# Two of the four gate stages moved behind attention segments, with gated activations in a ring of three

## The chip, the cores and the metric

The kernel runs on one core of a Trainium2 chip. The metric is the device time of one execution in microseconds (us). Before the change the median of three runs is 283.71 us (283.68 to 283.90).

## The reference, cut to what matters

Two branches read the same input x (2048 tokens of 512 features, bf16). Branch A is an attention with 32 heads of 16 features over four segments of 512 tokens. Inside a segment it is causal softmax attention. Beside it stands a memory: segment s reads what the keys and values of the segments before it have added up. Branch B is a gated feed-forward layer of width 1792. A gate per token mixes the two.

```
phi = lambda t: where(t > 0, t + 1.0, exp(t))
for s in range(4):
    p = softmax(qs @ ks.T * scale + mask);  a_dot = p @ vs
    a_mem = (phi(qs) @ M) / (phi(qs) @ z + 1e-6)
    o = g * a_mem + (1 - g) * a_dot
    M = M + phi(ks).T @ vs;  z = z + phi(ks).sum()
a = concat(o) @ wo
b = (gelu(x @ w_gate) * (x @ w_up)) @ w_down
out = sigmoid(x . gate_w) * a + (1 - sigmoid(x . gate_w)) * b
```

## The kernel before, in words

All weights and the transposed input `xT` lie in SBUF for the whole run. The work is cut into 1,076 small tasks, and each task has a name. The string `ORDER` at the top of the file lists every task once, in the order in which it is issued; `Sched.run` walks it. An engine executes its own tasks in that order, and waits where a task needs a result or a buffer that another engine has not yet given. Nothing else sets the order. A suffix `@A` or `@D` puts a copy on ACT or DVE.

The names that the text uses, with s the segment, and c a group of eight heads:

- `gt s.p` (L320, through `gate_pair`): two blocks of x @ w_gate, eight matmuls of 128x512 into one PSUM tile of 2 banks. `egt s.p` (L487, ACT): gelu of that tile into `G`. There are 7 of each per segment.
- `up s.h` (L320, `up_group`): four matmuls of x @ w_up into one bank. `eup` (L497, DVE) multiplies it into `G` in place. 14 per segment.
- `k`, `q`, `v` (L320, L422): the projections, four matmuls each, with a copy to SBUF on ACT or DVE (`ek`, `eq`, `ev`). `ko` (L334) is a second, masked copy of k.
- `lg n` (L574): the logits of slot n. A segment has 20 slots (5 for each c), so n runs from 0 to 79. A slot writes two PSUM tiles of 2 banks. `ex n a` and `ex n b` (L597, ACT) take exp of each into the ring `pT` of 12; `as n a/b` (L606, POOL) zero the masked triangle.
- `pv s.c e/o` (L626): probabilities times values; `epv` (L644, DVE) transposes it out of PSUM; `r`, `rg`, `n`, `m`, `o` (L654 to L670, DVE) normalize it, add the memory part and put the result into `xT`, in the place of the input.
- `E`, `Q`, `Em`, `ph` (L690 to L701; ACT, DVE, DVE, POOL): phi of k or q. `pk` (L730, SP) transposes phi(k) by DMA, `M` (L739) updates the memory, `mbd` and `zbd` (L761, L764) lay it out. `den` (L780) and `num` (L810) read it; `eden`, `rma`, `rmr`, `rmg`, `enum`, `nm` (L790 to L823, DVE) finish that.
- `dn s.t.*` (L834): G @ w_down for 128 tokens, in three pieces of 5, 5 and 4 matmuls. `wo` (L839) adds the attention's output to the same PSUM bank, `os` (L879, L881) scales it, `st` (L844) stores it.
- `gz`, `egz`, `zsp`, `g2`, `omz`: the mixing gate of all tokens.

PSUM is shared by two rings. The ring `lg` has three tiles of 2 banks; it serves `gt`, `lg` and the `dn` of the last segment. The ring `gen` has two tiles of 1 bank; it serves all other matmul groups. A tile is taken in the order of ORDER, and its next user waits until its reader on ACT or DVE is done.

Before the change the order has three parts. First come the first segment's projections and all 28 `gt` with their gelus, padded with some `up`. The first `ex` names all gelus in its dependencies, so ACT passes from gelu to exp once. `G` is one tile for all four segments. The weights of the gate (`wga`) and one small tile lie in a pool `ph1` that is closed at the task `opened`; the rings `T` to `pk` then take its memory. Second come the 80 slots, with `up`, projections, memory work and `dn` between them. Third, behind `lg79`, come the rest of the `dn` and `wo`.

The loads are issued by SP at the start, in this order: x of segment 0, `wk`, `wq`, the first part of `wga`, `wv`, the rest of `wga`, x of segments 1 to 3 by DMA transposes (L234, four per segment), `gw`, `beta8`, `wup`, `wo`. `wdn` follows as the first task on SP, because x of segment 0 first uses its place.

Of the kernel before, what the change touches and what calls it, by code (L numbers as in the profile page):

```python
# [32 lines left out]
open xt0 xt1 ext0 xt2 ext1 xt3 ext2 k0f0 ext3 k0f1 k0f2 q0.0 k0f3 eq0.0@D q0.1 ek0.1@A ek0.2@D  # L33
ek0.0@A gt0.0 eq0.1@A ek0.3@A gt0.1 egt0.0 q0.2 egt0.1 gt0.6 eq0.2@D gt1.3 gt1.0 egt1.3 egt0.6
q0.3 egt1.0 gt0.5 gt2.3 v0.0 egt2.3 gt1.1 egt0.5 eq0.3@A gt2.1 egt1.1 wdn gt1.6 egt2.1 gt0.3
egt1.6 gt0.2 egt0.3 v0.2 egt0.2 gt1.4 gt3.5 egt1.4 ev0.0@A ev0.2@A gt1.5 up0.6 egt1.5 gt3.0 eup0.6
egt3.5 gwB up0.10 gt3.3 eup0.10 up0.3 egt3.3 bps gt2.2 eup0.3 egt3.0 ebps omg gt1.2 egt2.2 up0.7
up0.4 eup0.7 gt2.5 eup0.4 eb gz ko0.0 egt2.5 ko0.1 gt3.6 egt1.2 egz zsp gt3.1 egt3.6 up0.2 egt3.1
gt2.0 up0.5 gt0.4 eup0.5 eup0.2 gt3.2 egt0.4 egt2.0 up0.0 gt2.4 eup0.0 gt3.4 egt2.4 egt3.2 up0.8
egt3.4 up0.1 eup0.8 gt2.6 eup0.1 wos v0.1 egt2.6 opened v0.3 ev0.1@D lg0 ev0.3@D up0.12 ex0a up0.9  # L40
eup0.12 up0.11 eup0.9 Ek0.0 up0.13 eup0.11 ex0b lg1 Qk0.0 eup0.13 q1.0 ex1a Emk0.0 k1.0 phk0.0
eq1.0@D ex1b lg2 ek1.0@D k1.1 ex2a ko1.0 v1.2 as0b pk0.0 ek1.1@D ex2b as0a lg3 as2a ev1.2@D q1.1
ex3a as1a v1.1 as1b Ek0.1 eq1.1@D as3a v1.3 ev1.1@A Emk0.1 Qk0.1 g2 v1.0 phk0.1 ev1.3@A ex3b lg4
ev1.0@D up1.0 ex4a up1.2 as2b pk0.1 eup1.0 Eq1.0 as4a up1.1 eup1.2 as3b ex4b Emq1.0 pv0.0e eup1.1
as4b lg5 epv0.0e M0.0 ex5a Qq1.0 up1.3 eM0.0 phq1.0 ex5b lg6 eup1.3 pv0.0o ex6a up1.4 epv0.0o as5b
ex6b as5a r0.0 up1.5 eup1.4 as6a Ek1.0 lg7 as6b eup1.5 M0.1 ex7a Qk1.0 up1.6 Emk1.0 eM0.1 ex7b lg8
ko0.2 rg0.0 up1.7 eup1.6 ex8a mbd0 as7b up1.8 eup1.7 ex8b lg9 as7a eup1.8 up1.9 as8a ex9a as8b
pv0.1e phk1.0 eup1.9 ex9b lg10 epv0.1e k1.2 ex10a k1.3 as9b ek1.2@D pk1.0 ex10b as9a q1.2 ek1.3@D
as10b Ek1.1 lg11 as10a eq1.2@D pv0.1o n0.0 ex11a up1.10 epv0.1o ex11b lg12 as11a eup1.10 q1.3
Emk1.1 ex12a Qk1.1 up1.11 phk1.1 eq1.3@A lg13 ex12b eup1.11 up1.12 omz ex13a r0.1 up1.13 as12b  # L50
eup1.12 pk1.1 Eq1.1 as11b up2.0 eup1.13 as12a ex13b lg14 eup2.0 pv0.2e ex14a Emq1.1 up2.1 ko0.3
epv0.2e ex14b lg15 rg0.1 Qq1.1 up2.2 eup2.1 ex15a as14b o0.0 up2.3 as13b eup2.2 ex15b as13a lg16
as14a eup2.3 up2.4 ex16a n0.1 pv0.2o eup2.4 ex16b as16a lg17 epv0.2o up2.5 ex17a as16b r0.2 up2.6
rg0.2 zbd0 eup2.5 ex17b as17a lg18 as15a eup2.6 up2.7 ex18a as15b n0.2 as17b up2.8 eup2.7 ex18b
phq1.1 lg19 eup2.8 pv0.3e ex19a o0.1 up2.9 epv0.3e ex19b lg20 as18a eup2.9 up2.10 as18b ex20a o0.2
as19a up2.11 as19b eup2.10 ex20b lg21 eup2.11 pv0.3o ex21a as20b up2.12 epv0.3o ex21b as21a r0.3
lg22 eup2.12 as20a up2.13 ex22a rg0.3 n0.3 den1 ex22b as22a eup2.13 lg23 as21b eden1 k2.0 ex23a
as22b o0.3 pv1.0e rma1 ek2.0@A as23a rmr1 ex23b lg24 num1.0 epv1.0e ex24a as23b rmg1 k2.1 enum1.0
ex24b ko1.1 lg25 nm1.0 q2.0 ex25a as24b ek2.1@D as24a eq2.0@D num1.1 ex25b lg26 enum1.1 pv1.0o
ex26a nm1.1 epv1.0o num1.2 ex26b as26a lg27 enum1.2 q2.1 ex27a nm1.2 as26b dn0.0.0 Ek2.0 as25a  # L60
lg28 as25b ex27b dn0.0.5 Emk2.0 as27a Qk2.0 ex28a as27b dn0.0.10 ko1.2 eq2.1@A phk2.0 wo0.0 ex28b
lg29 os0.0@D num1.3 ex29a enum1.3 pv1.1e as28b Eq2.0 lg30 as28a epv1.1e v2.0 as29a ex30a r1.0
Emq2.0 v2.1 ev2.0@D ex29b Qq2.0 v2.2 ev2.1@D ex30b as29b lg31 ev2.2@D v2.3 ex31a ko2.0 rg1.0
pv1.1o ev2.3@D ex31b lg32 epv1.1o M1.0 ex32a as31b r1.1 dn0.1.0 pk2.0 n1.0 as31a ex32b rg1.1 lg33
dn0.1.5 ex33a m1.0 as32b ko1.3 as30a ex33b lg34 st0.0 n1.1 dn0.1.10 as30b ex34a eM1.0 wo0.1 as32a
ex34b as34a lg35 os0.1@D pv1.2e ex35a as34b k2.2 epv1.2e as33a ex35b as33b lg36 ek2.2@D phq2.0
pv1.2o ex36a k2.3 epv1.2o ex36b lg37 ek2.3@D q2.2 as35b ex37a o1.0 as36b q2.3 eq2.2@D as35a ex37b
as36a lg38 eq2.3@D M1.1 as37a ex38a r1.2 as37b dn0.2.0 ko2.2 Ek2.1 eM1.1 lg39 dn0.2.5 ex38b Qk2.1
rg1.2 Emk2.1 n1.2 ex39a dn0.2.10 as38b ex39b lg40 as39a wo0.2 as38a ex40a as39b pv1.3e os0.2@D
phk2.1 ex40b lg41 epv1.3e st0.2 pv1.3o st0.1 ex41a up3.0 epv1.3o ex41b lg42 as41a eup3.0 up3.1  # L70
ko2.1 ex42a as41b up3.2 eup3.1 ex42b as42a lg43 eup3.2 up3.3 as40b ex43a mbd1 as42b up3.4 r1.3
eup3.3 ex43b as40a lg44 eup3.4 as43a pv2.0e ex44a rg1.3 m1.1 up3.5 epv2.0e Eq2.1 as44a o1.1 lg45
dn0.3.0 ex45a nm1.3 n1.3 ex44b dn0.3.5 zbd1 Emq2.1 m1.3 ex45b m1.2 as44b lg46 Qq2.1 dn0.3.10 ex46a
as43b eup3.5 wo0.3 phq2.1 o1.3 ex46b lg47 os0.3@D pv2.0o ex47a o1.2 st0.3 up3.6 as45a epv2.0o
ex47b as46b lg48 r2.0 den2 as46a ex48a eup3.6 as47b eden2 as45b ex48b lg49 as47a k3.0 rma2 ex49a
pv2.1e ek3.0@D ex49b lg50 as49a rmr2 k3.1 ex50a epv2.1e as49b ek3.1@D as48a num2.0 ex50b lg51
as48b enum2.0 pv2.1o rmg2 ex51a nm2.0 epv2.1o num2.1 ex51b lg52 enum2.1 q3.0 ex52a ko2.3 nm2.1
q3.1 eq3.0@D ex52b as52a lg53 eq3.1@D as50b num2.2 ex53a as51a enum2.2 dn1.0.0 as51b rg2.0 ex53b
as50a nm2.2 lg54 as53a dn1.0.5 ex54a n2.0 ex54b lg55 as54a dn1.0.10 as52b ex55a wo1.0 as53b as54b
Eq3.0 lg56 as55a os1.0@D pv2.2e ex56a m2.0 pv2.2o ko3.0 epv2.2e ex55b as56a epv2.2o num2.3 ex56b  # L80
lg57 as55b enum2.3 v3.0 r2.1 ex57a rg2.1 v3.1 n2.1 ex57b as57a ev3.0@D lg58 as56b ev3.1@D v3.2
ex58a as57b o2.0 ex58b lg59 ev3.2@D pv2.3e r2.2 m2.1 ex59a v3.3 epv2.3e ex59b lg60 ev3.3@D M2.0
rg2.2 ex60a dn1.1.0 eM2.0 n2.2 ex60b as60a lg61 Emq3.0 dn1.1.5 as59a Qq3.0 ex61a as58a dn1.1.10
o2.1 ex61b as58b nm2.3 as59b lg62 wo1.1 ex62a ko3.1 as61b pv2.3o os1.1@D ex62b lg63 as60b epv2.3o
st1.1 k3.2 as61a ex63a pk2.1 as62b k3.3 ek3.2@D as62a ex63b lg64 ek3.3@D pv3.0e ex64a as63b r2.3
as63a q3.2 st1.0 epv3.0e ex64b as64a lg65 eq3.2@D q3.3 ex65a as64b M2.1 eq3.3@A lg66 ex65b eM2.1
pv3.0o m2.2 ko3.2 dn1.2.0 ex66a rg2.3 epv3.0o as65b phq3.0 n2.3 ex66b lg67 dn1.2.5 ex67a dn1.3.0
as66a ex67b o2.2 lg68 as67a mbd2 dn1.2.10 ex68a as66b wo1.2 zbd2 Eq3.1 as68a r3.0 lg69 ex68b as67b
dn1.3.5 Emq3.1 m2.3 ex69a os1.2@D dn1.3.10 Qq3.1 ex69b st1.2 as69a lg70 rg3.0 wo1.3 as65a o2.3
ex70a as69b pv3.1e os1.3@D as68b ex70b lg71 epv3.1e st1.3 pv3.1o ex71a up3.7 epv3.1o n3.0 ex71b  # L90
lg72 up3.8 eup3.7 ex72a as71b up3.9 eup3.8 as70b ex72b as70a lg73 as71a eup3.9 up3.10 ex73a as72a
up3.11 as72b eup3.10 ex73b phq3.1 lg74 eup3.11 pv3.2e ex74a up3.12 epv3.2e ex74b as74a lg75
eup3.12 up3.13 as73b ex75a as74b den3 as73a eup3.13 ex75b as75a lg76 eden3 pv3.2o ex76a as75b rma3
dn2.0.0 r3.1 ko3.3 ex76b epv3.2o lg77 rg3.1 dn2.0.5 n3.1 ex77a as76b r3.2 rg3.2 dn2.0.10 ex77b
as77a rmr3 as76a lg78 wo2.0 as77b ex78a pv3.3e os2.0@D ex78b as78a lg79 epv3.3e st2.0 num3.0 ex79a
dn3.1.0 rmg3 enum3.0 ex79b as79a nm3.0 dn3.1.5 as78b dn3.2.0 m3.0 as79b dn3.2.5 num3.1 pv3.3o
enum3.1 dn3.0.0 epv3.3o nm3.1 dn3.0.5 o3.0 num3.2 dn2.1.0 enum3.2 m3.1 dn2.1.5 n3.2 r3.3 nm3.2
dn2.1.10 rg3.3 m3.2 wo2.1 num3.3 os2.1@A dn3.0.10 enum3.3 st2.1 o3.1 dn3.2.10 n3.3 dn2.2.0 nm3.3
dn3.1.10 m3.3 o3.2 dn2.3.0 o3.3 wo3.1 wo3.0 os3.1@D dn2.2.5 st3.1 os3.0@D wo3.2 dn2.3.5 os3.2@D
dn2.3.10 st3.2 st3.0 dn2.2.10 dn3.3.0 wo2.3 dn3.3.5 os2.3@D st2.3 dn3.3.10 wo2.2 wo3.3 os2.2@D  # L100
st2.2 os3.3@A st3.3
"""


class Task:


    __slots__ = ("name", "engs", "fn", "deps", "mode", "alloc", "frees", "kind", "cost", "prio")

    def __init__(self, name, engs, fn, deps=(), mode="full", alloc=(), frees=(), kind="",  # L110
# [39 lines left out]
def kernel(  # L150
# [45 lines left out]
    def gen(name):  # L196
        return pgen.tile([P, L], F32, name=name, tag="gen")

    pools = {}
    WP = ("T", "r", "N", "rm", "Tm", "Nm", "osb", "pkT", "pk")  # L200

    def rtile(ring, shape, dtype=BF, pool=None):
# [753 lines left out]
```

## Time and profile before

| what | us |
|---|---|
| median of three runs | 283.71 |
| the profiled execution: its time | 283.82 |
| its span, first to last instruction | 282.1 |
| busy: PE, ACT, DVE, POOL | 271.1, 204.2, 174.6, 125.9 |
| `lg0` starts, `lg79` starts | 74.8, 248.7 |

By stretch of the span, busy us of each engine, as the trace gives them:

| stretch (us) | PE | ACT | DVE | POOL |
|---|---|---|---|---|
| 11.2 to 74.8, gates of all segments | 63.28 of 63.60 | 32.22 | 12.08 | 5.23 |
| 74.8 to 129.6 | 53.44 of 54.80 | 50.31 | 45.62 | 35.11 |
| 129.6 to 183.9 | 52.65 of 54.30 | 52.67 | 44.91 | 35.76 |
| 183.9 to 239.0 | 53.01 of 55.10 | 53.05 | 45.20 | 34.86 |
| 249.3 to 282.1, behind the last slots | 28.61 of 32.80 | 3.19 | 16.10 | 2.22 |

Matmuls overlap: one of 128x512 is busy for 380 ns, and the next one starts 216 ns after it. So the steps from start to start, and not the busy share, tell how much of the time PE's work fills.

### The profile page before, as it was taken

The page shows a single profiled execution, that of the slowest core. Times are in us where ns is not written, and L with a number is a line of the kernel's source. Part 1 is how long each engine was busy: PE and PEld are TensorE (multiplying, and loading weights), DVE is VectorE, ACT ScalarE, POOL GpSimd, SP SyncE. Part 2 cuts the span into 40 slices and gives each one's busy share as a digit, 9 for nine tenths or more (in the row PEclk, how much of TensorE's full clock was granted, in tenths as well). Part 3 has the DMA queues.
Part 4 walks back from the last instruction along what each step waited for, and adds up shares of the span by engine and source line. Part 5 has one row for each costly group of instructions (what it writes and reads, how often), then busy time and mean ns, then how long its engine had stood idle before and what let it go on. Part 6 is the DMA issues. An engine that isn't in the chain of part 4 may idle for free.

```text
span 282.1 us, 5660 instructions
## 1 busy us (share of the span) xinstructions
PE 271.1 (96%) x2280; PEld 118.4 (42%) x2320; DVE 174.6 (62%) x324; ACT 204.2 (72%) x223; POOL 125.9 (45%) x220
## 2 busy tenths in 40 slices
PE   8999999999999999999899999999999999999994
PEld 4444444444444443444334444433444444344441
DVE  2100002510787878999969659989698877857721
ACT  3555654326689989999999999999999999950000
POOL 8000000060066686495575858584547657650000
PEclk9999999999999999999999999999999999999999
DMA  7973970000002211100001101000002000000011
GB/s 233 347 129 75 344 251 2 0 0 2 1 19 46 15 30 28 21 0 2 2 0 21 37 3 38 2 21 1 2 0 58 21 19 21 2 21 0 21 56 57
DMA packets 22019, 13.74 MB, mean 49 GB/s; under 512 B 14056, under 2 KB 20968, under 8 KB 21992
## 3 DMA queue, kind: packets, MB, share of 16 engines
q1 hardware_dynamic: 21448, 12.85, 16.8%
q10 hardware_dynamic: 544, 0.52, 0.5%
q8 instruction: 18, 0.29, 0.4%
q14 instruction: 9, 0.07, 0.1%
HBM read 8.13 MB, written 2.10 MB: 36 GB/s over the span
## 4 chain that ended last, share of the span: by engine, by line
PE 86%; DVE 8%; POOL 2%; issue 2%; DMA 1%; ACT 1%; SPq 0%; POOLq 0%
PE dn L834 18%; PE gt L320 17%; PE up L320 16%; PE lg L574 8%; PE pv L626 6%; PE dn L839 5%; PE q L320 4%; PE v L422 3%; PE k L320 3%; POOL pkT L701 2%; PE k L406 1%; PE M L739 1%; PE warm L371 1%; DMA pk<-pkT 1%; DVE T L644 1%
## 5 line engine op out<-in xcount | busy, mean ns | idle before, releaser
L597 ACT ACTIVATE pT<-lg 128x1024 bf16<-128x1024 f32 x160 | 153.4, 1032 | 8.2 <-PE lg L574 6.3
L606 POOL TENSOR_SCALAR_AFFINE_SELECT pT<-pT 128x512 bf16<-128x512 bf16 (+1 forms) x160 | 89.6, 588 | 54.7 <-ACT pT L597 52.4
L497 DVE TENSOR_TENSOR G<-up,G 128x512 bf16<-128x512 f32 x56 | 37.9, 683 | 52.5 <-PE up L320 49.2
L320 PE MATMUL up<-xT,wup 128*128 128x512 bf16 x211 | 54.0, 380 | 1.1 <-DVE G L497 0.5
L834 PE MATMUL dn<-wdn,G 128*128 128x512 bf16 x217 | 52.5, 380 | 0.5
L320 PE MATMUL gt<-xT,wga 128*128 128x512 bf16 x219 | 50.4, 379 | 0.3
L487 ACT ACTIVATE G<-gt 128x1024 bf16<-128x1024 f32 x28 | 27.7, 1023 | 31.1 <-PE gt L320 31.1
L320 PEld LDWEIGHTS <-wga 128*128 128x128 bf16 x224 | 21.8, 98 | 26.4 <-issue 0.4
L834 PEld LDWEIGHTS <-G 128*128 128x128 bf16 x224 | 20.6, 98 | 24.7 <-issue 2.4
L320 PEld LDWEIGHTS <-wup 128*128 128x128 bf16 x224 | 19.8, 97 | 25.6 <-issue 5.6
L458 POOL COPY G<-tt 32x16 f32<-32x16 f32 x16 | 3.2, 197 | 49.1 <-DVE tt L450 48.5
L644 DVE STREAM_TRANSPOSE T<-pv 128x512 f32<-128x512 f32 x32 | 22.5, 707 | 2.4 <-PE pv L626 2.3
L626 PE MATMUL pv<-pT,vz 128*32 128x256 bf16 (+2 forms) x640 | 23.2, 275 | 0.6 <-DVE osb L881 0.2
L881 DVE TENSOR_SCALAR osb<-dn,omz 128x512 bf16<-128x512 f32 x14 | 10.5, 750 | 19.6 <-PE dn L839 16.7
L701 POOL TENSOR_TENSOR pkT<-E,Q 128x1024 bf16<-128x1024 bf16 x6 | 12.8, 2128 | 21.1 <-PE q L320 18.6
L879 ACT ACTIVATE osb<-dn,omz 128x512 bf16<-128x512 f32 x2 | 1.4, 688 | 26.3 <-PE dn L839 26.3
L574 PE MATMUL lg<-qT,kT 16*128 16x256 bf16 (+2 forms) x320 | 17.9, 273 | 0.4
L574 PE MATMUL lg<-qT,kO 32*128 32x128 bf16 (+2 forms) x320 | 17.9, 272 | 0.0
L626 PEld LDWEIGHTS <-vz 128*32 128x32 bf16 x640 | 12.6, 96 | 11.1 <-issue 2.3
L320 PE MATMUL q<-xT,wq 128*128 128x512 bf16 x58 | 15.8, 380 | 1.0 <-DVE T L644 0.7
L839 PE MATMUL dn<-wo,xT 128*128 128x512 bf16 x62 | 15.7, 380 | 0.0
L422 PE MATMUL v<-wv,xT 128*128 128x512 bf16 x61 | 15.3, 379 | 0.2
(88 smaller groups left out, 244.7 us busy)
## 6 DMA issues: line engine op xcount, KB each, us to landing
out_dram<-osb SPq DMA_DIRECT2D x16, 128.0 KB, 1.7
wup<-in_B_w_up_dram SPq DMA_DIRECT2D x1, 1792.0 KB, 8.1
wdn<-in_B_w_down_dram SPq DMA_DIRECT2D x1, 1792.0 KB, 13.6
wga<-in_B_w_gate_dram SPq DMA_DIRECT2D x1, 1280.0 KB, 10.7
wq<-in_A_wq_dram SPq DMA_DIRECT2D x1, 512.0 KB, 6.1
wga<-in_B_w_gate_dram SPq DMA_DIRECT2D x1, 512.0 KB
wv<-in_A_wv_dram SPq DMA_DIRECT2D x1, 512.0 KB, 8.0
wo<-in_A_wo_dram SPq DMA_DIRECT2D x1, 512.0 KB, 9.1
```

Source lines behind the costliest of these rows:

```text
L320: nc.tensor.matmul(t, lhsT=W[:, fc, c0:c0 + P], rhs=xT[:, fc, s * L:(s + 1) * L], start=(fc == 0), stop=(fc == FC - 1))
L422: nc.tensor.matmul(t[:, :], lhsT=xT[:, fc, s * L + kt * P:s * L + (kt + 1) * P], rhs=wv[:, fc, :], start=(fc == 0), stop=(fc == FC - 1))
L487: ge = evac("ACT", g, box, lambda e, t: nc.scalar.activation(dst, t[:, :, :], AF.Gelu_apprx_tanh), kind="gelu", ring="lg")
L497: UPT[(s, hs)] = evac("DVE", g, box, lambda e, t: nc.vector.tensor_mul(G[:, s, hs, :], t[:, :], G[:, s, hs, :]), kind="up")
L574: nc.tensor.matmul(A[j // 2][:, j % 2, at * P:(at + nq) * P], lhsT=l, rhs=r, start=True, stop=True, tile_position=(32 * j, 0))
L597: nc.scalar.activation(pT[(s, t, h)][:, :, :], A[h][:, :, :], AF.Exp, scale=0.25)
L606: nc.gpsimd.affine_select(out=v, in_=v, pattern=pat, compare_op=ALU.is_ge, fill=0.0, base=0, channel_multiplier=-1)
L626: nc.tensor.matmul(t[32 * j:32 * j + 32, qb * P:(qb + nq) * P], lhsT=vz[s % 2][:, kt, h * VW:h * VW + 32], rhs=pT[(s, t0 + w, j // 2)][:, ...
L644: nc.vector.transpose(TT[key][:, e, :, :].rearrange("p a b -> p (a b)"), t[:, :])
L701: nc.gpsimd.tensor_add(d[:, :, :], box["E"][:, :, :], box["Q"][:, :, :])
L834: nc.tensor.matmul(t[:, :], lhsT=G[:, s, hs, qt * P:(qt + 1) * P], rhs=wdn[:, hs, :], start=(hs == 0), stop=stop and (hs == HS - 1))
L839: nc.tensor.matmul(t, lhsT=xT[:, c, s * L + qt * P:s * L + (qt + 1) * P], rhs=wo[:, c, :], start=first and c == 0, stop=(c == NCH - 1))
```

## The change

The order is new. The gates of segments 0 and 1 stay at the start; those of segment 2 stand behind slot 19, where the attention of segment 0 ends, and those of segment 3 behind slot 39. This adds changes of ACT's function table: `egt` needs the gelu table, `ex`, `E` and `g2` the exp table. In the compiled program ACT has 3 table loads before and 13 after: one more pair round `Ek0.1` in the first part, three pairs behind slot 19 (round `Ek1.1` and `Eq1.1` too) and one behind slot 39. Some of the loads carry the semaphore wait of the activation behind them; so do those ahead of `Ek1.1` and `Eq1.1` (they wait for DVE).

`G` becomes a ring of three tiles of one segment each. `egt3.0` takes the tile of segment 0, and so waits for all `dn0.*`. `wga` stays in SBUF for good, the pool `ph1` and the task `opened` are gone, and `tt` uses the ring `Tm`. `wup`, `gw` and `beta8` are now loaded ahead of x of segments 1 to 3; `wdn` is issued behind `pk1.1`. The numbers of matmuls, activations and DMAs are otherwise the same.

```diff
-    G = ctile("G", [P, NSEG, HS, L])
+    wga = ctile("wga", [P, FC, DFF])
+    G = {}
...
     nc.sync.dma_start(wga[:, :, 4 * P:DFF], wgr[:, :, 4 * P:DFF])
+    load_w(nc.sync, wup, B_w_up)
+    nc.sync.dma_start(gw[:, :], gate_w.rearrange("(fc p) -> p fc", p=P))
+    nc.sync.dma_start(beta8[:, :], A_beta.rearrange("(c h) -> h c", h=8))
     for s in range(1, NSEG):
         load_x(s)
-    nc.sync.dma_start(gw[:, :], gate_w.rearrange("(fc p) -> p fc", p=P))
-    nc.sync.dma_start(beta8[:, :], A_beta.rearrange("(c h) -> h c", h=8))
-    load_w(nc.sync, wup, B_w_up)
     load_w(nc.sync, wo, A_wo)
...
+        def fn(_, t):
+            if hp == 0:
+                G[s] = rtile("G", [P, HS, L])
+            nc.scalar.activation(G[s][:, 2 * hp:2 * hp + 2, :], t[:, :, :], AF.Gelu_apprx_tanh)
...
+    for s in range(2, NSEG):
+        GM[(s, 0)].deps.append(XT_[((s - 1) * NSLOT - 1, 1)])
+        for hp in range(HS // 2):
+            GG[(s, hp)].deps.append(LT[(s - 1) * NSLOT - 1])
```

The new order round slot 19 and round slot 39, as far as the text speaks of it:

```
lg19 eup1.10 up1.11 as16b ex19a Qq1.0 k1.2 Emq1.0 n0.1 phq1.0 ex19b gt2.0
eup1.11 k1.3 egt2.0 as15a as19b gt2.2 ek1.3@D as15b ek1.2@D as19a o0.0 as18a Ek1.1 pv0.3e as18b
omz pv0.3o ko1.1 rg0.2 gt2.1 epv0.3o epv0.3e egt2.2 o0.1 q1.2 Qk1.1 Emk1.1 q1.3 r0.3 phk1.1 eb
egt2.1 gt2.3 eq1.2@D eq1.3@D rg0.3 M0.1 wos Eq1.1 gt2.4 pk1.1 eM0.1 n0.3 zbd0 mbd0 up1.12 egt2.3
n0.2 gt2.5 wdn Emq1.1 o0.3 eup1.12 egt2.4 gt2.6 Qq1.1 phq1.1 egt2.5 lg20 egt2.6 up1.13 ex20a den1
...
lg39 up2.11 ... gt3.0 ... pv1.3e pv1.3o gt3.1 k2.3 up2.12 dn0.3.0 dn0.2.0 dn0.2.5 dn0.2.10
dn0.3.5 dn0.3.10 gt3.4 egt3.0 wo0.2 egt3.1 wo0.3 gt3.3 gt3.2 M1.1 gt3.5 gt3.6 den2 lg40
```

(The lines on slot 39 leave out most tasks of the other engines.)

## The prediction

> **What bounds the kernel.** I read the page's slices, then the chain of waits, then PE's timeline.
>
> ```profile
> span 282.1 us, 5660 instructions
> PE 271.1 (96%) x2280; PEld 118.4 (42%) x2320; DVE 174.6 (62%) x324; ACT 204.2 (72%) x223; POOL 125.9 (45%) x220
> ...
> PE   8999999999999999999899999999999999999994
> ...
> ACT  3555654326689989999999999999999999950000
> ...
> PE 86%; DVE 8%; POOL 2%; issue 2%; DMA 1%; ACT 1%; SPq 0%; POOLq 0%
> ```
>
> PE is busy from end to end, ACT is nearly full only in the slots, and the chain that ends last runs 86% through PE and 1% through ACT. Busy matmuls overlap, so I take steps from start to start. In this stretch of PE's timeline (start, us, line, operation, operands, count) both kinds of step are seen.
>
> ```profile
> 190.19 0.40 PE L574 MATMUL lg<-qT,kT 16*128 16x256 bf16 x12
> 190.52 0.73 PE L626 MATMUL pv<-pT,vz 128*32 128x512 bf16 x20
> 191.18 0.39 PE L810 MATMUL num<-pq,Mbd 128*128 128x512 bf16 x1
> 191.50 0.58 PE L574 MATMUL lg<-qT,kT 16*128 16x256 bf16 x4
> 191.81 0.39 PE L574 MATMUL lg<-qT,kO 32*128 32x256 bf16 x4
> 192.60 1.89 PE L320 MATMUL q<-xT,wq 128*128 128x512 bf16 x7 [0.40 <-DVE T L644]
> 194.42 0.40 PE L574 MATMUL lg<-qT,kO 32*128 32x512 bf16 x4
> ```
>
> A slot's logits take 0.33 us, a `pv` 0.66, eight matmuls 1.82 (eight times 0.216, and 0.095 where a smaller tile follows). At 192.60 PE has lost 0.76: DVE had not emptied a `gen` tile. Adding all steps: 940 matmuls by 0.216 is 203.0; 80 slots by 0.329 is 26.3; 32 `pv` 21.0; `M`, `num`, warm-up and the other small groups 10.9; 83 changes to a smaller tile by 0.095 is 7.9. Together **269.1 us**. Span 282.1 is 1.3 ahead of PE's first matmul, 269.1 of work, **7.6 us of waits**, and 4.1 from the last issue to the end. Only the 7.6 can be won: 1.8 up to `lg20`, 2.4 to `lg40`, 3.1 in segment 2 and 0.3 behind it. PE's long tail behind `lg79` (29 us) is no loss: it is dense.
>
> **The change part by part.** *PE's work.* Each matmul stays. Two more pairs of `pv` stand together (0.16 saved on each) and one change of tile is added: 269.1 - 0.3 + 0.1 = 268.9, so -0.2 us. The gates' 28 by 1.73 us are only moved.
>
> *ACT.* Ten table loads are added.
>
> ```profile
> 73.17 1.02 ACT L487 ACTIVATE G<-gt 128x1024 bf16<-128x1024 f32 x1 [2.33 <-PE gt L320]
> 74.21 1.28 ACT L597 ACT_TABLE_LOAD   x1
> 75.50 1.02 ACT L597 ACTIVATE pT<-lg 128x1024 bf16<-128x1024 f32 x1
> ...
> 81.36 1.94 ACT L597 ACTIVATE pT<-lg 128x1024 bf16<-128x1024 f32 x2 [0.23 <-PE lg L574]
> ```
>
> Gelu to load 1.04, load to exp 1.29: 2.33 instead of the 0.92 between the two exps at 81.36, so 1.41 more per change, 14.1 in all. They cost nothing while PE has work and PSUM tiles: a gate takes PE 1.73 us and ACT 0.92. If that cover were gone entirely, it would be the 14.1. Weighed against the Trainium skill, "ScalarE: Activation LUTs", section "What ACT_TABLE_LOAD costs" (and its rule to group calls by table set, which speaks against this change): it gives 1283 ns for the load, as the row has, and a drain of about 1380 ns more, where the row shows some 0.1 us. By 2.66 us per change, my estimate behind slot 19 would grow by about 2.5 us, to some 285.4 in all.
>
> *Start.* PE queue: `k0f3`, `q0.0`, then `gt0.0` at 10.4. Six gates later ACT takes exp for `Ek0.1` and back: `egt0.3` ends at 22.8, load, `Ek0.1` (1.0), load, `egt0.4` ends at 27.4; its tile is wanted by `gt1.5` at 27.7. It just fits. All other tiles are free 1 us or more ahead. `lg0` starts at about 40 in place of 74.8, with 0.1 of waits. SP: `wup` (1792 KB) and `gw` now lie ahead of x of segment 1, which `gt1.0` wants at 24.2. In the old trace 1280 KB of `wga` land by 14.2; `wup`'s packets then ran at 0.39 MB per us (so 4.7 us, to 18.7), `gw` took 1.9, the transposes 0.5 each: x1 at 22.6 to 23.5. Costed at 0; bound: 0 to 2.5 (four transposes at 1.26 apart behind `gw`, and the 1.5 us to land that the last x1 to x3 needed).
>
> *Segment 0.* Between slots stand two `up` or an `up` and a `pv`: 1.95 to 2.15 us per slot for PE against 1.84 for two exps; DVE has 1.3 us per slot. Cover is better than before, where segment 0's 1.8 us of waits came from DVE. One new wait: `zsp` (32 copies, 16 by 0.144 and 16 by 0.222 apart, 5.9 us) now stands on POOL in slot 8, ahead of 5 selects that `pv0.1o` wants at 8.7 us past `lg8`; they end at 9.1. With small ones: 0.8.
>
> *Behind slot 19* (times from `lg19`; matmul steps as above, DVE at 0.6 per 512-column operation, as two transposes stand 0.6 apart, 0.33 per bf16 one). PE: `up1.11`, `k1.2`, `gt2.0` to 3.8, `k1.3`, `gt2.2` to 6.4, `pv` twice to 7.7, `gt2.1` to 9.4, `q1.2`, `q1.3`, `gt2.3` to 12.95, `M0.1`, `gt2.4`, `up1.12`, `gt2.5` to 17.7. ACT: `egt2.0` 4.0 to 4.9; the load ahead of `Ek1.1` waits for DVE's `ek1.2` (6.1), so `Ek1.1` ends 8.4, `egt2.2` 10.75, `egt2.1` 11.65; the load ahead of `Eq1.1` waits for `eq1.3` (13.3), so `egt2.3` ends 17.95. `gt2.6` needs that tile: waits 0.35. `lg20` at 19.9 (dense 19.4): 0.45 lost. Behind `lg20`, `den1` waits 0.1 for POOL's `phq1.1` (19.0 to 21.1, behind `Qq1.1`), `up2.1` 0.2 for `eden1`, and the `num` chain of DVE (`rmr` 0.94, `enum`, `nm`) costs PE 0.95 by `lg24` and 0.5 more by `lg27`: 1.75, like the 1.8 it cost before from `lg24` on. To `lg39` 0.5 more.
>
> *Behind slot 39.* PE has 26.3 us here (six `dn0` pieces and two `wo0` too), ACT 11. `egt3.0` waits for `dn0.3.10` (14.7) and ends 15.75; its tile is wanted by `gt3.3` at 18. `zbd1` ends 0.35 ahead of `den2`. Cost 0.1; if the cover goes, as behind slot 19. The `num` chain then 1.6, the rest of segment 2 0.6 (3.1 before: its `v3`, `num` and `dn` now have `up3` between them).
>
> *Segment 3.* New: `den3`, `num3`, and two `os2` on ACT fall into the slots. `os2.0` holds `ex72a` until 2.85 past `lg71`, PE has only 0.99 in slot 72: 0.5; twice 0.3 behind it. 1.1 in all, where nothing was lost. Tail: `pv3.3e` at 4.75 past `lg79`, POOL's selects for it end at 4.3; nine `dn3` pieces cover the last DVE chain. 0.2, as before.
>
> Sum of waits: 0.1 + 0.8 + 0.45 + 1.75 + 0.5 + 0.1 + 1.6 + 0.6 + 1.1 + 0.2 = 7.2; against 7.6: -0.4, and -0.2 of work. I take 0.2 more off, since queue walks of the old segment 1 gave 0.8 for a wait of 0.63 (`num1.0` to `k2.1`). 283.82 - 0.8 = 283.0; the median lies 0.1 under the profiled run: **282.9 us**. The unknown costs: table changes behind a wait -0 to +14.1 (I take the row's 1.41, mostly covered), x1 0 to 2.5, DVE below.
>
> **The rivals.** (1) *Nothing won*: the waits behind the slots 19 and 39 and in segment 3 take what segments 0 and 2 give back: 283.1 to 284.3. For it: the sum above differs by less than its terms' errors. (2) *Slower: the chain behind slot 19 becomes the bound.* DVE's 24 operations up to `eq1.3` are counted at their step; at their mean durations (about 0.08 more each: 0.69 for a cast that steps 0.6) they end 1.9 us later, and `Eq1.1`, two loads, `egt2.3`, `gt2.6` and `lg20` follow one for one: it decides from `eq1.3` ending later than 12.95. Then `phq1.1` delays `den1` by as much again: 0.35 + 1.9 + 1.0, less what is in my sum: 285 to 286.5. Against it: DVE runs back to back at its steps elsewhere. (3) *x1 late*: `gt1.0` waits up to 2.5, nothing behind it has slack to give back: 284.3 to 285.4. (4) *Nearly all waits go*, 281.3 or less: bounded below by 283.8 - 7.8 = 276. Against it: the `num` chain is still there.
>
> **Numbers.** My forecast (281.3 to 283.1) 0.42, rival 1 0.25, rival 2 0.24, rival 3 0.06, rival 4 0.03. Faster by over 0.2% (0.57 us, about what can be told from no change) is forecast and rival 4: 0.45; same 0.25; slower 0.30. For 8 in 10 the range runs from 281.3 to 286.0; the forecast's own is 281.3 to 283.1.
>
> **What would show it.** Right: `lg0` near 40, 13 table loads of 1.28 us, PE's steps unchanged, waits of `num`, `k` and `v` on DVE still there, ACT idle in the tail for a shorter time. Wrong: a gap of PE of over 1 us ahead of `gt2.6` or `lg20` with ACT as releaser; PE waiting for a DMA near 24 us; many short waits of `lg` on ACT in slots 20 to 27 and 40 to 50, which would mean that two exps take more than I counted.

## The result, and the profile after

The changed kernel takes 285.26 us (median; 284.88 to 285.46), the kernel before 283.78 beside it: ratio 1.0050, interval 1.0033 to 1.0068. Run again later: 285.11, ratio 1.0053 (1.0039 to 1.0066). So it is **slower by 0.5%**, where 0.3% faster was forecast. The profiled execution took 284.88 (span 283.2), the lowest of its runs.

The lines of its page that answer to those shown of before:

```profile
span 283.2 us, 5710 instructions
PE 273.3 (97%) x2320; PEld 117.3 (41%) x2320; DVE 169.9 (60%) x323; ACT 219.5 (78%) x234; POOL 121.7 (43%) x220
...
PE   7999999999999899999999999899999999999994
...
ACT  3549779889998599999992577999989999977110
...
PE 85%; DVE 9%; ACT 3%; POOL 1%; issue 1%; ACTq 0%; DVEq 0%; POOLq 0%
```

ACT's exps now begin in the sixth slice instead of the eleventh, and ACT's idle tail is shorter; PE is still the bound. The dip of ACT to 5 in the fourteenth slice (92 to 99 us) is the place to look at. There the timelines (start, us, engine, line, operation, operands, count, and in brackets the idle time ahead of it with its releaser) show, first PE:

```profile
94.44 1.89 PE L313 MATMUL gt<-xT,wga 128*128 128x512 bf16 x8
97.35 0.63 PE L731 MATMUL M<-vz,pk 128*128 128x136 bf16 x8 [1.03 <-DVE qT L176]
...
100.41 1.89 PE L313 MATMUL gt<-xT,wga 128*128 128x512 bf16 x8
102.71 1.89 PE L313 MATMUL gt<-xT,wga 128*128 128x512 bf16 x8 [0.41 <-ACT G L481]
```

`gt2.3` at 94.44 should be followed 1.72 us later; `M0.1` comes 2.91 later, so PE lost 1.19 for a `gen` tile that DVE's cast `eq1.2` had not emptied. `gt2.6` at 102.71 lost 0.57 for the tile of `egt2.3`. Why was the cast late? DVE, and beside it POOL:

```profile
93.82 0.12 DVE L507 RECIPROCAL ebr<-omg 128x4 f32<-128x4 f32 x1
93.97 1.95 DVE L508 TENSOR_SCALAR ebr<-ebr 128x4 f32<-128x4 f32 x1
95.96 0.74 DVE L510 TENSOR_SCALAR bdeb<-bd,ebr 128x128 bf16<-128x128 bf16 x4
96.61 1.28 DVE L176 CAST qT<-q 128x512 bf16<-128x512 f32 x2
```

```profile
93.78 2.12 POOL L693 TENSOR_TENSOR pkT<-E,Q 128x1024 bf16<-128x1024 bf16 x1 [3.72 <-issue]
```

The second operation of `eb` works on four numbers per partition and took 1.95 us. In before, where `eb` stood elsewhere, it took 0.17:

```profile
53.04 0.17 DVE L515 TENSOR_SCALAR ebr<-ebr 128x4 f32<-128x4 f32 x1
```

In the changed kernel it starts 0.19 behind POOL's addition of `phk1.1` and ends at 95.92, 0.02 behind that addition's end at 95.90. Both casts stand behind it. ACT pays too:

```profile
97.97 1.28 ACT L682 ACT_TABLE_LOAD   x1 [2.86 <-DVE qT L176]
99.27 1.06 ACT L682 ACTIVATE E<-qT 128x1024 bf16<-128x1024 bf16 x1
100.34 1.28 ACT L481 ACT_TABLE_LOAD   x1
101.64 4.02 ACT L481 ACTIVATE G<-gt 128x1024 bf16<-128x1024 f32 x4
```

ACT stood idle for 2.86 us ahead of the load for `Eq1.1`, which carries the wait for `eq1.3`; behind it come `Eq1.1`, a second load and only then `egt2.3`.

Before had the same once, unseen by me: `omz` (128x16) took 0.88 us and ended with an addition of POOL,

```profile
109.83 0.88 DVE L468 TENSOR_SCALAR omz<-omz 128x16 f32<-128x16 f32 x1
```

```profile
108.55 2.12 POOL L701 TENSOR_TENSOR pkT<-E,Q 128x1024 bf16<-128x1024 bf16 x1 [0.88 <-DVE Q L694]
```

and PE waited 0.62 us ahead of `up2.0`:

```profile
111.80 1.02 PE L320 MATMUL up<-xT,wup 128*128 128x512 bf16 x4 [0.46 <-DVE G L497]
```

The table sets out PE's waits in us, each the step from one group to the next less the same step where nothing waits (so a warm-up shorter than counted gives a value below 0). The last column is the time as a ratio to before with its interval. The labels stand with the experiments below.

| kernel | to lg0 | lg0-19 | lg19-20 | lg20-39 | lg39-40 | lg40-46 | lg46-69 | from lg69 | ratio |
|---|---|---|---|---|---|---|---|---|---|
| before | 0.14 | 1.80 | 0.01 | 2.37 | 0.01 | 0.06 | 3.05 | 0.30 | 1 |
| changed | 0.02 | 0.57 | **1.86** | 2.01 | 0.34 | 2.11 | 0.76 | 1.32 | 1.0050 (1.0033-1.0068) |
| changed, again | 0.17 | 0.62 | **1.87** | 1.99 | 0.34 | 2.11 | 0.77 | 1.32 | 1.0053 (1.0039-1.0066) |
| 1 `eb` in slot 7 | 0.73 | **1.98** | 0.10 | 2.00 | 0.34 | 2.10 | 0.76 | 1.31 | 1.0036 (1.0025-1.0048) |
| 2 `eb` ahead of the addition | 0.33 | 0.59 | 0.10 | 2.03 | 0.34 | 2.11 | 0.76 | 1.31 | 0.9988 (0.9979-0.9997) |
| 3 no gelu table | 0.44 | 0.58 | 1.30 | 2.00 | 0.34 | 2.10 | 0.76 | 1.31 | 1.0028 (1.0019-1.0037) |
| 4 before, `omz` moved | -0.03 | 1.18 | 0.01 | 2.37 | 0.01 | 0.06 | 3.05 | 0.30 | 0.9982 (0.9971-0.9992) |
| 5 addition on DVE | 0.65 | 0.57 | 0.10 | 1.99 | 0.33 | 2.11 | 0.76 | 1.32 | 0.9988 (0.9979-0.9997) |
| 6 addition in two | 0.55 | 0.62 | 1.74 | 2.00 | 0.34 | 2.11 | 0.76 | 1.32 | 1.0047 (1.0033-1.0061) |
| 7 `os2` on DVE | 0.37 | 0.59 | 1.86 | 2.00 | 0.34 | 2.11 | 0.76 | 1.72 | 1.0057 (1.0042-1.0072) |
| 8 = 2 + 7 | 0.36 | 0.57 | 0.10 | 2.04 | 0.34 | 2.10 | 0.76 | 1.73 | 1.0003 (0.9994-1.0012) |
| 9 = 8 + `num2.3` later | 0.37 | 0.59 | 0.11 | 2.04 | 0.34 | 1.77 | 0.90 | 1.73 | 0.9997 (0.9988-1.0006) |
| 10 = 9 + `num1.3` later | -0.25 | 0.59 | 0.10 | 2.35 | 0.34 | 1.77 | 0.90 | 1.73 | 1.0005 (0.9995-1.0015) |
| 11 = 2 + `num2.3` later | 0.14 | 0.62 | 0.10 | 2.04 | 0.34 | 1.77 | 0.90 | 1.32 | 0.9978 (0.9968-0.9988) |

Changed less before: waits 9.0 against 7.7, matmul work 0.2 less, so 1.1 more of span, as measured (283.2 against 282.1). Segment 0 and slots 46 to 69 give back 3.5 us of waits; behind slots 19, 39 and 40 and from `lg69` on 5.2 are new. The first column differs from run to run of one and the same start (loads landing, a cast). That may be why the profiled execution lies 0.4 below its median; no trace of the median run shows it.

### The profile page after: what moved, and what is told of

Same layout as the page of the kernel before. It is cut to its first block, busy times and chain, and to the rows that moved or that the text cites. A ratio compares the mean times of both kernels' runs of the same rounds, so it can differ in the third digit from the quotient of the medians.

```text
span 283.2 us, 5710 instructions
## 1 busy us (share of the span) xinstructions
PE 273.3 (97%) x2320; PEld 117.3 (41%) x2320; DVE 169.9 (60%) x323; ACT 219.5 (78%) x234; POOL 121.7 (43%) x220
## 4 chain that ended last, share of the span: by engine, by line
PE 85%; DVE 9%; ACT 3%; POOL 1%; issue 1%; ACTq 0%; DVEq 0%; POOLq 0%
PE dn L826 17%; PE up L313 16%; PE gt L313 15%; PE lg L567 8%; PE pv L618 7%; PE v L415 5%; PE dn L831 5%; PE q L313 4%; PE k L313 3%; DVE G L490 3%; PE k L399 1%; ACT pT L590 1%; PE M L731 1%; DVE T L636 1%; PE den L772 1%; DVE qT L176 1%
## 5 line engine op out<-in xcount | busy, mean ns | idle before, releaser
L599 POOL TENSOR_SCALAR_AFFINE_SELECT pT<-pT 128x512 bf16<-128x512 bf16 (+1 forms) x160 | 84.6, 556 | 84.1 <-ACT pT L590 82.6
L313 PE MATMUL up<-xT,wup 128*128 128x512 bf16 x224 | 55.7, 380 | 1.0 <-DVE kT L176 0.5
L313 PE MATMUL gt<-xT,wga 128*128 128x512 bf16 x224 | 51.3, 379 | 0.4 <-ACT G L481 0.4
L693 POOL TENSOR_TENSOR pkT<-E,Q 128x1024 bf16<-128x1024 bf16 x6 | 12.9, 2146 | 46.2 <-DVE Q L686 24.1
L176 DVE CAST qT<-q 128x512 bf16<-128x512 f32 x14 | 9.6, 689 | 21.9 <-PE q L313 21.8
L873 DVE TENSOR_SCALAR osb<-dn,omz 128x512 bf16<-128x512 f32 x9 | 6.8, 751 | 24.6 <-PE dn L831 19.7
L693 POOL TENSOR_TENSOR pq<-E,Q 128x1024 bf16<-128x1024 bf16 x6 | 13.1, 2185 | 12.0 <-DVE Q L686 10.6
L871 ACT ACTIVATE osb<-dn,omz 128x512 bf16<-128x512 f32 x7 | 4.8, 687 | 15.1 <-PE dn L831 15.1
L415 PE MATMUL v<-wv,xT 128*128 128x512 bf16 x64 | 16.0, 380 | 0.0
```

The lines of the kernel that those rows point to most:

```text
L313: nc.tensor.matmul(t, lhsT=W[:, fc, c0:c0 + P], rhs=xT[:, fc, s * L:(s + 1) * L], start=(fc == 0), stop=(fc == FC - 1))
L415: nc.tensor.matmul(t[:, :], lhsT=xT[:, fc, s * L + kt * P:s * L + (kt + 1) * P], rhs=wv[:, fc, :], start=(fc == 0), stop=(fc == FC - 1))
L599: nc.gpsimd.affine_select(out=v, in_=v, pattern=pat, compare_op=ALU.is_ge, fill=0.0, base=0, channel_multiplier=-1)
L693: nc.gpsimd.tensor_add(d[:, :, :], box["E"][:, :, :], box["Q"][:, :, :])
```

## The experiments

The theory T: `eb`'s small operation is held up by POOL's addition. Its main rival R: the added table loads on ACT make the stage behind slot 19 late.

**1. `eb` in slot 7** (label e1_eb_early)

```diff
-... as6b omg as6a ...  ... phk1.1 eb egt2.1 ...
+... as6b omg eb as6a ...  ... phk1.1 egt2.1 ...
```

> The changed kernel with one word moved: `eb` stands directly behind `omg` in slot 7 instead of behind `phk1.1`; nothing else is touched. Theory T: in the changed kernel `eb`'s small multiplication (128x4, line 508) took 1.95 us on DVE because it ran beside POOL's addition of `phk1.1` and ended with it; `eq1.2`, `eq1.3`, then `M0.1` on PE and, over ACT's `Eq1.1`, `egt2.3` and `gt2.6` were late by that. So both waits of PE in that stretch (1.19 and 0.57 us) go: 1.4 to 1.8 us less than the changed kernel's 285.3, 283.5 to 283.9, ratio to before about 1.000. Rival R (the added table loads on ACT behind slot 19 are the cause): no change, 285.0 to 285.5.

Measured: 284.67 us, against 285.11 and 285.26 of the changed kernel: a miss in the time. Behind slot 19 all of it came true (1.86 to 0.10), with every table load still there: R alone can't be the cause. But a new wait of 1.39 us stands ahead of `up1.0` in slot 8. PE, DVE and POOL there:

```profile
61.17 1.02 PE L312 MATMUL up<-xT,wup 128*128 128x512 bf16 x4 [1.32 <-DVE G L489]
```

```profile
58.23 0.18 DVE L506 RECIPROCAL ebr<-omg 128x4 f32<-128x4 f32 x1
58.44 0.34 DVE L507 TENSOR_SCALAR ebr<-ebr 128x4 f32<-128x4 f32 x1
58.82 1.70 DVE L509 TENSOR_SCALAR bdeb<-bd,ebr 128x128 bf16<-128x128 bf16 x4
60.44 0.68 DVE L489 TENSOR_TENSOR G<-up,G 128x512 bf16<-128x512 f32 x1
```

```profile
57.54 2.77 POOL L598 TENSOR_SCALAR_AFFINE_SELECT pT<-pT 128x512 bf16<-128x512 bf16 x5 [2.56 <-ACT pT L589]
```

I had moved `eb` from beside an addition to beside five selects: its four multiplications took 1.70 instead of 0.74, and `eb` as a whole 2.2 (58.23 to 60.44) instead of 1.0. The multiplication that empties `up0.13`'s tile stands behind it. So by these figures about 1.2 of the 1.39 are the same kind of hold-up, in smaller pieces, at another place, and the rest is `eb`'s own work.

**2. `eb` ahead of the addition** (label e2_eb_ahead_of_add)

```diff
-... o0.1 q1.2 Qk1.1 Emk1.1 q1.3 r0.3 phk1.1 eb egt2.1 ...
+... o0.1 eb q1.2 Qk1.1 Emk1.1 q1.3 r0.3 phk1.1 egt2.1 ...
```

> The changed kernel with `eb` moved ahead of `q1.2 Qk1.1 Emk1.1`, so that DVE has the same operations to do ahead of `eq1.2` as in the changed kernel, but none of `eb`'s runs beside POOL's addition of `phk1.1`. T: `eb`'s 128x4 multiplication takes about 0.17 us instead of 1.95, and most of the gain of the run with `eb` in slot 7 comes: 283.5 to 284.2. A rival to T (DVE has too many operations there, whichever they overlap): as the changed kernel, 285.0 to 285.5. R: the same, 285.0 to 285.5.

Measured: 283.48 us, 0.9988 of before: **1.6 to 1.8 us less than the changed kernel, by one word moved six tasks up.** DVE and PE:

```profile
93.42 0.17 DVE L507 TENSOR_SCALAR ebr<-ebr 128x4 f32<-128x4 f32 x1
...
95.22 1.22 DVE L175 CAST qT<-q 128x512 bf16<-128x512 f32 x2
96.36 0.98 DVE L648 TENSOR_TENSOR r<-r,G 128x32 f32<-128x32 f32 x1
```

```profile
94.77 1.89 PE L312 MATMUL gt<-xT,wga 128*128 128x512 bf16 x8
96.50 0.64 PE L730 MATMUL M<-vz,pk 128*128 128x136 bf16 x8
...
99.56 3.62 PE L312 MATMUL gt<-xT,wga 128*128 128x512 bf16 x15
```

The operation takes 0.17, `M0.1` follows `gt2.3` at the dense step (1.73), and `gt2.5` and `gt2.6` run through. DVE's list ahead of the casts is the same, so it was not too full. The casts, which read PSUM, ran beside the addition unhurt; `rg0.3` (128x32, two SBUF inputs) is now the one held up, 0.98 instead of 0.18, where nobody waits.

**3. No gelu table** (label e4_no_gelu_table)

```diff
-            nc.scalar.activation(G[s][:, 2 * hp:2 * hp + 2, :], t[:, :, :], AF.Gelu_apprx_tanh)
+            nc.scalar.activation(G[s][:, 2 * hp:2 * hp + 2, :], t[:, :, :], AF.Exp)
```

> The changed kernel with the gates' gelu replaced by exp, so that ACT changes its function table once instead of 13 times; the gelu is left out of what is computed. T: ACT saves 12 changes of about 1.41 us, but of PE's waits behind slot 19 only the one for `egt2.3` ahead of `gt2.6` (0.57 us) goes; `M0.1`'s 1.19 us stays, because it waits for DVE: 284.2 to 284.9. R: the whole excess behind slot 19 (1.86 us) and more goes: 282.5 to 283.4.

Measured: 284.60 us, in T's range. PE:

```profile
94.87 1.89 PE L313 MATMUL gt<-xT,wga 128*128 128x512 bf16 x8
97.79 0.63 PE L731 MATMUL M<-vz,pk 128*128 128x136 bf16 x8 [1.03 <-DVE qT L176]
...
100.85 3.62 PE L313 MATMUL gt<-xT,wga 128*128 128x512 bf16 x15
```

Twelve table changes of 1.41 us are gone, 17 us of ACT's time, and PE gets 0.57 back: the wait of `gt2.6`. `M0.1`'s stays to the hundredth, and so do 2.0 behind `lg20` and 2.10 behind `lg40`. That is what the loads cost the kernel here, and only behind the late `eq1.3`: in experiment 2 they are all there and that wait is gone.

**4. The same in the kernel before** (label e5_before_omz)

```diff
-... Qk1.1 up1.11 ...  ... phk1.1 eq1.3@A lg13 ...  ... up1.12 omz ex13a ...
+... Qk1.1 omz up1.11 phk1.1 ...  ... eq1.3@A lg13 ...  ... up1.12 ex13a ...
```

> The kernel before with `omz` moved to directly behind `Qk1.1` and `phk1.1` moved behind `up1.11`, so that DVE's 128x16 operation of `omz` no longer runs beside POOL's addition of `phk1.1`. In the trace of before it took 0.88 us and ended with that addition; PE waited 0.62 us behind it ahead of `up2.0`. T: the operation takes about 0.13 us, that wait goes, and the kernel is 0.3 to 0.6 us faster than before: ratio 0.998 to 0.999. Rival (such an operation is only slow by itself there): same time as before, its duration stays near 0.9 us.

Only `omz` moved (`phk1.1` stood behind `up1.11` already). Measured: 283.10 us, 0.9982 (0.9971 to 0.9992). As T has it:

```profile
108.07 0.17 DVE L466 TENSOR_SCALAR omz<-omz 128x16 f32<-128x16 f32 x1
```

0.17 us instead of 0.88, and PE's 0.62 ahead of `up2.0` is gone. This makes the comparison fairer: with the costliest collision taken out of each kernel, the order of the change (0.9988) and that of before (0.9982) can't be told apart. Others are left in both: an operation of 2.47 us in before (last section), at no cost to PE, and one ahead of `pv1.0o` in experiment 2 (see experiment 10).

**5. The addition on DVE** (label e8_add_on_dve)

```diff
-            nc.gpsimd.tensor_add(d[:, :, :], box["E"][:, :, :], box["Q"][:, :, :])
+            eng = nc.vector if name == "k1.1" else nc.gpsimd
+            eng.tensor_add(d[:, :, :], box["E"][:, :, :], box["Q"][:, :, :])
```

> The changed kernel with one addition, that of `phk1.1`, on DVE instead of POOL; the order is that of the changed kernel, `eb` behind it. T (`eb` is held up by POOL's addition): its 128x4 multiplication takes about 0.17 us instead of 1.95, DVE pays some 0.75 us for the addition itself (twice the 0.41 of the 128x512 bf16 addition of line 659, less overlap), `eq1.3` is 1.0 us earlier, and most of PE's 1.19 and 0.57 us go: 283.7 to 284.4. Rival (the operation is slow at that place whatever POOL does): DVE only gets more to do, 285.8 to 286.3.

Measured: 283.31 us, 0.9988: better than expected.

```profile
94.45 0.63 DVE L694 TENSOR_TENSOR pkT<-E,Q 128x1024 bf16<-128x1024 bf16 x1
95.00 0.16 DVE L507 RECIPROCAL ebr<-omg 128x4 f32<-128x4 f32 x1
95.20 0.17 DVE L508 TENSOR_SCALAR ebr<-ebr 128x4 f32<-128x4 f32 x1
```

Nothing has moved in the order, DVE has one more operation, and `eb` takes 0.17: so it is POOL's addition, not the place. DVE does in 0.63 us, stepping 0.55, what took POOL 2.12 and held DVE up for 1.8.

**6. The addition in two halves** (label e10_add_in_two)

```diff
-            nc.gpsimd.tensor_add(d[:, :, :], box["E"][:, :, :], box["Q"][:, :, :])
+            for i in range(0, 2) if name == "k1.1" else [slice(None)]:
+                nc.gpsimd.tensor_add(d[:, i, :], box["E"][:, i, :], box["Q"][:, i, :])
```

> The changed kernel with POOL's addition of `phk1.1` cut into two of half the size, one behind the other; `eb` stays behind it in the order. If a DVE operation that reads and writes SBUF waits for the POOL instruction that is under way to end, and not for POOL's work as a whole, `eb`'s operations get in between the halves: the 128x4 multiplication ends with the first half, at about 1.0 instead of 1.95 us, the next may wait for the second half. If it is let in for good there: 284.0 to 284.6. If DVE waits for the second half too: as the changed kernel, 285.0 to 285.5.

Measured: 285.30 us, as the changed kernel. DVE, then POOL:

```profile
94.56 0.98 DVE L508 TENSOR_SCALAR ebr<-ebr 128x4 f32<-128x4 f32 x1
95.58 1.59 DVE L510 TENSOR_SCALAR bdeb<-bd,ebr 128x128 bf16<-128x128 bf16 x4
```

```profile
94.36 2.27 POOL L694 TENSOR_TENSOR pkT<-E,Q 128x512 bf16<-128x512 bf16 x2 [3.69 <-issue]
```

The small operation ends at 95.54, when POOL's two are half over (95.5); the four behind it take 1.59 instead of 0.74 and pay for the second half. So DVE is held for one POOL instruction at a time and gets in between two; but as long as it has another such operation, it is held again.

**7 and 8. `os2.0` and `os2.1` on DVE** (labels e3_os_on_dve, best_eb_os)

```diff
-os2.0@A ... os2.1@A
+os2.0@D ... os2.1@D
```

> The changed kernel with `os2.0` and `os2.1`, the evacuations of two output tiles, on DVE instead of ACT; `eb` stays where the change has it. In the changed kernel PE waits 0.37 us ahead of `lg72`, 0.24 ahead of `lg73` and 0.26 ahead of `num3.2`, just behind these two. If ACT's place in the order (two evacuations between exps that are already back to back) is what PE waits for there: 0.6 to 0.9 us less than the changed kernel, 284.4 to 284.7. Rival (DVE, which takes them over, is as full there): no change, 285.0 to 285.5.

> The changed kernel with `eb` ahead of `q1.2 Qk1.1 Emk1.1` and `os2.0`, `os2.1` on DVE: the two edits together. The waits that they take away lie in stretches 130 us apart, so the gains should add: 1.8 us for `eb` (measured: 285.26 to 283.48) and 0.6 to 0.9 for the two evacuations: 282.6 to 282.9, ratio to before 0.996 to 0.997. If the second edit gains nothing alone, 283.3 to 283.7.

Measured: 285.44 and 283.88 us; no gain alone, and a small loss on top of experiment 2 (283.48). A miss. PE's line in the changed kernel, then the two of experiment 7:

```profile
244.21 0.73 PE L618 MATMUL pv<-pT,vz 128*32 128x512 bf16 x20 [0.30 <-ACT osb L871]
```

```profile
244.56 0.73 PE L617 MATMUL pv<-pT,vz 128*32 128x512 bf16 x20 [0.30 <-DVE osb L872]
...
246.54 1.67 PE L825 MATMUL dn<-wdn,G 128*128 128x512 bf16 x6 [0.39 <-DVE T L635]
```

What waits is not `lg72` for `ex72a` but `pv3.1o` for the `gen` tile of `wo2.0`: with `num3.0` between them, three groups want two tiles, whichever engine empties them. On DVE, `os2.0` also delays `enum3.0`, and `dn2.1.0` pays 0.4 for that.

**9, 10 and 11. `num2.3` and `num1.3` later** (labels e6_num2_later, e7_num1_later, e9_best)

```diff
-... ex44a nm2.2 as43b ...  ... ex45a enum2.3 q3.0 ...     (num2.3 ahead of ex45a)
+... ex44a as43b ...  ... ex45a q3.0 ...  ... dn1.0.5 nm2.2 num2.3 enum2.3 ex48a ...
```

Experiment 10 also has `eq2.0@D`, and `num1.3 enum1.3` behind `dn0.0.5`. Experiment 11 is experiment 2 with the edit above and `os2` on ACT.

> The kernel with both edits, and `nm2.2`, `num2.3`, `enum2.3` moved from slots 44 and 45 to slot 48, where DVE is nearly idle (0.08 us of work in 3.8). Behind `lg40` DVE is busy for 11.1 of 13.1 us and PE waits 2.1 us for it. If DVE's own work is what bounds that stretch: 1.5 us less of it, and PE's waits there fall by 0.5 to 0.9 (ACT's exps, 12 of 0.97 behind a table load, allow no more): 281.8 to 282.4 from 282.7. Rival (ACT's table load and exps are what PE waits for there): less than 0.2 us.

> As the kernel with `num2.3` in slot 48, and the same for segment 1: `num1.3`, `enum1.3` one slot later (behind `dn0.0.5`) and `eq2.0` on DVE in their place instead of ACT. PE waits 0.53 us ahead of `num1.3` in the changed kernel, for the PSUM tile that ACT's copy `eq2.0`, queued behind exps, gives back late. If so: 0.3 to 0.5 us less than the kernel without this edit. Rival: `pv1.0o` takes the wait over, no change.

> `eb` ahead of `q1.2 Qk1.1 Emk1.1`, and `nm2.2`, `num2.3`, `enum2.3` in slot 48; `os2.0` and `os2.1` stay on ACT. The first edit alone gave 283.48, ratio 0.9988. The second, seen in the traces, brings `lg46` 0.53 us earlier and `lg69` 0.17, which then stays. Expected 283.2 to 283.4, ratio 0.997 to 0.999.

Measured: 283.73, 284.10 and 283.22 us. DVE behind `lg40` in the changed kernel, where these start:

```profile
176.29 0.94 DVE L789 RECIPROCAL rm<-rm 128x128 f32<-128x128 f32 x1
177.15 1.22 DVE L490 TENSOR_TENSOR G<-up,G 128x512 bf16<-128x512 f32 x2
178.29 0.28 DVE L792 TENSOR_TENSOR rm<-rm,G 128x128 f32<-128x128 f32 x1
178.49 0.71 DVE L811 STREAM_TRANSPOSE Tm<-num 128x512 f32<-128x512 f32 x1
179.23 0.69 DVE L815 TENSOR_TENSOR Nm<-Tm,rm 128x512 bf16<-128x512 f32 x1
179.84 0.68 DVE L176 CAST kT<-k 128x512 bf16<-128x512 f32 x1
```

No idle time is noted for any of them, and PE's waits there name DVE:

```profile
178.43 1.02 PE L313 MATMUL k<-xT,wk 128*128 128x512 bf16 x4 [0.22 <-DVE G L490]
...
180.58 1.02 PE L313 MATMUL up<-xT,wup 128*128 128x512 bf16 x4 [0.48 <-DVE kT L176]
```

Taking 1.5 us of DVE's work out lowered the waits of that stretch from 2.10 to 1.77 and `lg46` came 0.5 us earlier, but `num2.3`'s own matmul and a wait of 0.14 came back later, and 0.17 is left at `lg69`: expected 0.3 to 0.9, a miss. By size alone the rival (less than 0.2) fits; that the waits of the stretch fell with DVE's work, and stay at 2.10 without the table load (experiment 3), speaks for DVE. The times can't tell this from nothing in experiment 9 (0.9997 against 1.0003); the traces do.

Experiment 10 gained nothing, and its premise was a misreading. In the changed kernel the 0.53 stand ahead of `pv1.0o`, not of `num1.3`, and what releases PE is DVE's `eup2.4`, not ACT's `eq2.0`:

```profile
118.63 0.39 PE L802 MATMUL num<-pq,Mbd 128*128 128x512 bf16 x1
119.47 0.73 PE L618 MATMUL pv<-pT,vz 128*32 128x512 bf16 x20 [0.45 <-DVE G L490]
```

```profile
117.06 1.16 DVE L815 TENSOR_TENSOR Nm<-Tm,rm 128x512 bf16<-128x512 f32 x1
```

`eup2.4` is late behind this operation, which has two SBUF inputs, usually takes 0.68 and here runs beside POOL's selects. `up2.4`'s matmuls end at 118.37 and `eup2.4` starts at 118.77, so some 0.4 of the 0.53 would be the same hold-up once more (an estimate; no run moves it). In experiment 10 `pv1.0o` waits 0.84, for `eq2.0` on DVE behind that same operation.

Experiment 11, **283.22 us, 0.9978 (0.9968 to 0.9988)**, is in its range and beats both kernels; it is not measurably better than before with `omz` moved.

## Why the prediction was wrong

- **The step that failed** stands under *Behind slot 19*: "the load ahead of `Eq1.1` waits for `eq1.3` (13.3)" and "0.45 lost", with DVE "at 0.6 per 512-column operation". `eq1.3` ended 14.6 us past `lg19`, `M0.1` (dense at 12.95) waited 1.19 for `eq1.2`, which I did not have at all, and `gt2.6` 0.57 instead of 0.35: 1.86 instead of 0.45. `eb`, moved beside POOL's addition, ran from 93.82 to 96.61, 2.8 us; where nothing holds it up, 1.0, and `eq1.3` ends 12.8 past `lg19` (experiment 2). I costed each engine's operations as if the engines only met through semaphores. Rival 2 named the place and the point ("from `eq1.3` ending later than 12.95"), and its range (285 to 286.5) holds the result; but it put the delay down to DVE's mean durations. DVE kept its steps, and one operation was held up. Its chain ran as far as `gt2.6` and no further: `den1` was not late by as much again. The 285.4 in the prediction's part on ACT lies near the result by luck: a table change took about as long as in the old trace (2.37 for 2.33), and taking twelve out gave PE 0.57.
- **The `num` chain behind `lg40`**: forecast 1.6, measured 2.11. The mechanism was right (DVE back to back), the size was not; ACT's load has no part in it (experiment 3).
- **Segment 3**: forecast 1.1, measured 1.09 up to `lg79`, but not by my mechanism: `gen` tiles, not `ex72a` behind `os2.0`. A right number for a wrong reason; the edit that followed from the reason (experiment 7) failed.
- **Right**: PE's work (269.1 to 268.9); `lg0` at 39.9; segment 0 in size (0.57 for 0.8, though `pv0.1o`, where `zsp` was to cost some of it, did not wait); `lg20` to `lg39` in size (2.01 for 2.25, of which some 0.4 at `pv1.0o` is a hold-up too); the rest of segment 2 (0.76 for 0.6, where before lost 3.05); the tail; 13 table loads, at about 1.4 more per change (99.27 to 101.64 is 2.37, against 0.92); x1, which landed at 22.9, ahead of `gt1.0` at 24.1. Behind slot 39 0.34 for 0.1.
- The sum: 1.41 (behind slot 19) + 0.51 (`lg40`) + 0.24 (behind 39) - 0.4 (the others) is 1.8 more waits than the forecast's 7.2. With `eb` out of the way the waits are 7.6 and the median 283.48, still 0.6 above my number: what I took off beyond the sum (0.2) and the `num` chain are the rest.

## What to carry to other kernels

Where an order is changed, look for what newly runs at the same time on DVE and POOL, not only at each engine's queue: a 0.17 us operation on SBUF data can take almost as long as the POOL instruction that it meets. Read one duration of an operation against its other durations in the trace; a long one that ends together with another engine's instruction may have been held by it, and moving one of the two shows whether it was. And before crediting or blaming a reordering, take the costly accidents out of both kernels: here they were larger than the effect of the order.

## What the runs showed of the hardware

In these traces, a `tensor_scalar` of DVE from SBUF to SBUF, or an operation with two SBUF inputs, that begins after POOL's addition never ends before it. Its time goes from 0.17 us alone to 1.95 beside the addition (128x4), from 0.13 to 0.88 (128x16), from 0.18 to 0.98 (128x32, two inputs) and from 0.69 to 2.47 (128x512, two inputs, in before). Beside POOL's shorter selects such operations are slowed: from 0.35 to between 0.5 and 0.7 for `kO` 128x512, from 0.74 to 1.70 for `eb`'s four. Not held up beside the addition: casts from PSUM (0.62 to 0.70), multiplications with one PSUM input (0.65 to 0.69), DVE's 32x32 transposes (0.67 to 0.72), and `reciprocal` (0.12 in `eb`). Where DVE began first, it was POOL that took longer: beside `n0.1`, which starts at 84.80 and keeps its 0.68, the addition that starts at 84.96 took 2.49 instead of 2.12 (changed kernel).

The Trainium skill, "SBUF — State Buffer", section "🔬 SBUF: two separate sides", has this: the port pair that DVE and GpSimd share is an exclusive lock, and whoever starts first keeps it for the whole instruction. The runs agree: 1.95 us with the whole addition, 0.98 with half of it, and 2.49 for the addition that came second. I had not weighed that page in the prediction.
